# Reordered steps in the four later chunks of an mLSTM cell followed by a GELU MLP

## The chip, the cores and the metric

The kernel runs on one core of one Trainium2 chip. The metric is the device time of one execution in microseconds (us), from the kernel's start on the core to its end. It is written in Bass with the Tile framework, but its order is its own: the tile pools and semaphores are Tile's, while every instruction stands on its engine's queue in the order in which the program issues it (`tc.manual_schedule()`). Five engines have such a queue: PE (TensorE: matrix products and transposes), DVE (VectorE), ACT (ScalarE), POOL (GpSimd) and SP (SyncE, which here only starts DMA transfers). An engine takes its queue strictly in order; a wait for another engine is a semaphore in front of the instruction that waits.

## What is computed

Two blocks, one behind the other. The first is an mLSTM cell on 4 batches, 8 heads, 768 time steps and head size 40:

```python
C, n, m = 0, 0, -1e30
for t in range(768):                      # every batch and head
    m_new  = max(f[t] + m, i[t])
    f_stab = exp(f[t] + m - m_new)
    i_stab = exp(i[t] - m_new)
    C = f_stab * C + i_stab * outer(v[t], k[t])
    n = f_stab * n + i_stab * k[t]
    h = C @ q[t]
    y[t] = sigmoid(o[t]) * h / max(abs(n . q[t]), 1)
    m = m_new
```

Its output, 3072 tokens of 320 numbers (8 heads x 40), goes through an MLP: `h = x @ w_in` (320 to 2048), `g = 0.5 * h * (1 + erf(h / sqrt(2)))`, `out = g @ w_out` (2048 to 320), all in float32.

## The kernel before, in words

*The cell.* The 768 steps are cut into six chunks of 128. Within a chunk the recurrence is written as matrix products: scores of keys with queries, weighed by a matrix W of exponentials (with a mask), times the values; to that comes a product of the queries with the state that the chunk before has left. Of each chunk the four batches (0 to 3) are handled one by one or in pairs (0, 1 and 2, 3).

*The MLP.* A chunk makes 512 tokens (4 batches x 128). They are multiplied by w_in in four groups of four tiles of 128 hidden features (16 tiles); each tile goes through the GELU, and then the 16 tiles are multiplied by w_out and summed in four PSUM accumulators, one per batch. To keep the precision of float32, operands are split: `x_hi`, `x_rest`, `x_low` for the input (six products for the up projection), a whole and two parts for g (three products for the down projection).

*The interleaving.* Chunk 0's MLP has a form of its own. For chunks c = 1 to 5 the MLP of chunk c is mixed with the cell of chunk c + 1, so that TensorE has matrix products of the MLP to do while the other engines work on the cell. The order is written out by hand, in strings of words; `play()` (L1019) runs through the string from left to right and issues each word's instructions, on whichever engines it uses. A word is a letter and a number: the batch, or the tile or group of the MLP. A batch number of 4 or more belongs to the cell one chunk further on (M4 is the mask of batch 0 of cell c + 2). SECOND is played for chunk 1, LATER for chunks 2, 3 and 4, and LAST for chunk 5, which has no cell beside it. Because each engine's queue is in program order, a word's place in the string is its place on every engine that it uses, and two words which share no engine don't order one another.

The words that matter here, with their engine, their lines and what they write:

| word | what it does | engine, line |
|---|---|---|
| U, u | up projection of a group, first part and rest | PE L966, L977, into `pu` |
| g | GELU of one tile: `g_whole`, a part, difference, cast | ACT L984, L985; DVE L986, L987 |
| d | down projection of one tile, 12 matmuls, all four batches | PE L991, into `po` |
| E | output of the chunk before: copy out of `po`, send | ACT L1015 to `o_sb`; SP |
| K, Q | transposes of keys, queries | DVE L512 |
| M, W | mask; exponentials | POOL L474; ACT L500 |
| G | output gate, tanh | ACT L506 |
| D | values times their weights | POOL L539 |
| C0, h0 / C2, h2 | read the state for a pair; update the state for the pair | PE L621 (64 matmuls); PE L632 (32), DVE L639 and L647, POOL L643 |
| S0, S2 | scores of a pair, 64 matmuls; weighing by W | PE L568; DVE L574 |
| V0 to V3 | values of one batch, 64 matmuls, and the sum with the state's part | PE L674 into `ph`; DVE L678 |
| Y | the division and the gate | DVE L685 to L690 |
| t | copy of the last 64 columns of y, twice | ACT L699 |
| X | transpose of y for the MLP ("turn") and its first part | PE L708 (3 transposes) into `px`; ACT L718 to `x_hi` |
| R | `x_rest` and `x_low` from `px` and `x_hi` | DVE L727, L728 |
| L, B, J, O, j, o | loads of blocks of keys and queries, of W's exponents, and of keys, values, gates | SP |
| + | next of the copies of keys and queries to a DRAM scratch `kq_d` | SP |
| Z, a, b | pieces of the splitting of w_in and w_out | ACT, DVE |

*What sets the order around the change.* Dependences that an order must keep: C2 needs the transposed queries (Q2, Q3) and the state; h2 needs the weighed values (D2, D3) and stands behind C2, whose banks `pf` it shares; V2 and V3 need the scores' products (S2) and write into the banks that S0's scores used, and their sum on DVE needs h2's `far`; Y needs V; t and X need Y; X2 and X3 write `px` into the banks of C2 and h2; R needs X. The next chunk's U0 reads `x_hi`, `x_rest` and `x_low` of all four batches. The banks that S2 and C2 write are ones that the up projection's groups use too, so that they must wait until the last GELU of a group (g11, g15) has read its bank. The buffers of g's parts are reused after some tiles, so a g waits for an earlier d.

In code the two steps that the change moves furthest on TensorE, `later_values` (V) and `update_two` (h), are:

```python
for hip in range(2):
    for p in range(NP):
        for r in quarters:
            nc.tensor.matmul(ph[hip][r, p, :], Pm[:, 2 * p + hip, r], vb[turn_of(n)][:, 2 * p + hip, :], ...)
```

```python
nc.tensor.matmul(banks[i][used[hip], H + p, :], k_later[turn_of(c * B + b)][:, 2 * p + hip, :], vw[:, 2 * p + hip, :], ...)
```

The functions that play the strings, with their lines:

## Time and profile before

| what | value |
|---|---|
| time, median of 3 runs | 438.67 us (437.14 to 439.19) |
| the profiled execution: its time, its span | 438.46 us, 436.7 us |
| PE matmuls, busy | 427.3 us, 98% of the span, 5472 instructions |
| PE weight loads, busy | 374.6 us, 86% |
| DVE busy | 296.0 us, 68% |
| ACT busy | 277.3 us, 63% |
| POOL busy | 48.8 us, 11% |
| granted TensorE clock | 1.00, the whole span |

How to read the profile. One execution was recorded. The *span* is from the first to the last recorded instruction; the time of the execution is longer by what lies around it, 438.46 - 436.7 = 1.8 us here. *Busy* time is the time in which an engine has an instruction at work; PEld is the loading of weights into TensorE's array, which overlaps the matmuls (PE). A row of the *groups* gives a line of the kernel, engine, operation, output <- inputs with their sizes, how many, and the mean time. The *chain of waits* goes back from the last instruction, at each step to what released it, and so shows what carries the end; shown in order of time, a row is start, length, engine, tile, line and count, in us. A row "issue" is time in which an engine waited for nothing that the profile shows. The *timeline* lists single instructions, or runs of equal ones, in a stretch of time: start, duration, engine, line, operation; in square brackets stands the idle time before it and what ended it. The *table by stretches* has one row for a stretch from A to B: its length, then the busy time and, in brackets, the number of instructions of PE, PEld, DVE, ACT and POOL, then the granted clock, the busy share of the DMA engines and GB/s. PEldq is the queue of TensorE's instructions, as its sequencer works it off.

### The profile page before, as it was taken

To read this page: it belongs to the slowest core of one execution; us is meant where nothing else is said; L and a number is where in the kernel's file an instruction comes from. 1 tells how busy PE (TensorE), PEld (TensorE's weight loads), DVE (VectorE), ACT (ScalarE), POOL (GpSimd) and SP (SyncE) were. 2 spreads that over 40 slices of the span, in tenths; PEclk is the share of its full clock that TensorE was granted. 3 is DMA by queue.
4 is the path that set the end of the run, shared out by engine and by line. 5 is a ranking of instruction groups with operands and counts; after the bars stand their busy time and mean duration, and the time that the engine had idled before them with its cause. 6 is when DMAs were issued, how large, how long until landed. Compare 5 with 4: busy or idle time off the path is not lost.

```text
span 436.7 us, 13291 instructions
## 1 busy us (share of the span) xinstructions
PE 427.3 (98%) x5472; PEld 374.6 (86%) x5472; DVE 296.0 (68%) x680; ACT 277.3 (63%) x595; POOL 48.8 (11%) x77
## 2 busy tenths in 40 slices
PE   8989999999999999999999999999999999999996
PEld 7777888877988899988899988899988889979986
DVE  8797687797888697747597747597746586533330
ACT  4989999856889985228785229785247715243441
POOL 3001030000430041030041030040010000000000
PEclk9999999999999999999999999999999999999999
DMA  7999994577791592662492653571561400010001
GB/s 151 220 214 243 233 256 87 138 211 179 229 154 56 106 176 60 115 179 50 84 187 42 123 158 60 117 134 32 110 156 17 62 2 2 22 42 2 1 2 60
DMA packets 162268, 48.83 MB, mean 112 GB/s; under 512 B 147776, under 2 KB 155232, under 8 KB 162208
## 3 DMA queue, kind: packets, MB, share of 16 engines
q1 hardware_dynamic: 161888, 47.65, 50.1%
q8 instruction: 43, 0.70, 0.6%
q10 hardware_dynamic: 320, 0.33, 0.2%
q14 instruction: 17, 0.14, 0.1%
HBM read 43.84 MB, written 9.37 MB: 122 GB/s over the span
## 4 chain that ended last, share of the span: by engine, by line
PE 73%; DVE 2%; ACT 2%; DMA 1%; issue 1%; ACTq 0%
PE po L991 31%; PE pu L966 24%; PE pu L977 7%; PE ps L568 3%; PE pf L621 2%; PE ph L674 1%; PE po L888 1%; PE po L674 1%; PE px L708 1%; DMA bits<-in_moe_w_out_dram 1%; PE pf L632 1%; DVE pow L416 1%; DVE w_out L419 0%; ACT w_out_part L935 0%; ACT g_part L873 0%
## 5 line engine op out<-in xcount | busy, mean ns | idle before, releaser
L991 PE MATMUL po<-w_out_part,g_parts 128*128 128x320 f32 x960 | 140.7, 303 | 0.0
L991 PEld LDWEIGHTS po<-w_out_part,g_parts 128*128 128x128 f32 x960 | 131.6, 189 | 5.9 <-issue 4.6
L986 DVE TENSOR_TENSOR g_parts<-g_whole,g_parts 128x512 fp32r<-128x512 f32 x80 | 57.0, 713 | 58.1 <-ACT g_parts L985 56.0
L984 ACT ACTIVATE g_whole<-pu 128x512 f32<-128x512 f32 x80 | 47.1, 589 | 74.2 <-PE pu L977 63.7
L985 ACT ACTIVATE g_parts<-g_whole 128x512 fp32r<-128x512 f32 x80 | 50.5, 631 | 8.3 <-PE po L991 5.1
L474 POOL TENSOR_SCALAR_AFFINE_SELECT W<-W 128x1024 f32<-128x1024 f32 (+2 forms) x20 | 21.7, 1088 | 189.2 <-DMA W<-M_d 154.4
L500 ACT ACTIVATE W<-W,aT 128x128 f32<-128x128 f32 x128 | 38.8, 389 | 0.3
L987 DVE CAST g_parts<-g_whole 128x512 fp32r<-128x512 f32 x80 | 36.2, 453 | 0.0
L699 ACT COPY far<-ob 128x128 f32<-128x128 f32 x16 | 4.6, 290 | 32.9 <-DVE ob L690 32.9
L966 PE MATMUL pu<-x_hi,w_in_hi 128*128 128x512 f32 x80 | 24.2, 384 | 0.0
L966 PE MATMUL pu<-x_hi,hi_first 128*128 128x512 f32 x80 | 24.0, 381 | 0.1
L966 PE MATMUL pu<-x_rest,hi_first 128*128 128x512 f32 x80 | 23.8, 379 | 0.0
L966 PE MATMUL pu<-x_rest,w_in_hi 128*128 128x512 f32 x80 | 23.8, 379 | 0.0
L966 PE MATMUL pu<-x_low,w_in_lo 128*128 128x512 f32 x80 | 23.8, 379 | 0.0
L966 PE MATMUL pu<-x_low,w_in 128*128 128x512 f32 x80 | 23.8, 379 | 0.0
L888 PE MATMUL po<-w_out,g 128*128 128x320 f32 x80 | 22.0, 432 | 0.0
L404 ACT ACTIVATE sig<-bits 128x320 f32<-128x320 f32 (+1 forms) x26 | 15.2, 586 | 10.4 <-issue 6.1
L574 DVE TENSOR_TENSOR W<-ps,W 128x256 f32<-128x256 f32 (+1 forms) x48 | 17.7, 414 | 4.2 <-PE ps L568 3.2
L888 PEld LDWEIGHTS po<-w_out,g 128*128 128x128 f32 x80 | 15.0, 190 | 5.9
L639 DVE TENSOR_TENSOR far<-pf,gT 128x164 f32<-128x164 f32 x32 | 8.4, 319 | 16.1 <-PE pf L632 11.7
L416 DVE SCALAR_TENSOR_TENSOR pow<-sig,pow 128x320 uint32<-128x320 uint32 (+1 forms) x26 | 15.4, 592 | 4.3 <-ACT pow L405 4.3
L1015 ACT ACTIVATE o_sb<-po 128x320 f32<-128x320 f32 x20 | 7.5, 443 | 16.7 <-PE po L991 16.7
(196 smaller groups left out, 778.9 us busy)
## 6 DMA issues: line engine op xcount, KB each, us to landing
W<-M_d SPq DMA_DIRECT2D x16, 512.0 KB, 6.5
bits<-in_moe_w_in_dram SPq DMA_DIRECT2D x20, 256.0 KB, 4.2
bits<-in_moe_w_out_dram SPq DMA_DIRECT2D x16, 320.0 KB, 4.6
blocks<-kq_d SPq DMA_DIRECT2D x32, 128.0 KB, 3.5
ob<-in_o_gate_dram SPq DMA_DIRECT2D x24, 160.0 KB, 4.1
out_dram<-o_sb SPq DMA_DIRECT2D x36, 80.0 KB, 2.0
wide<-M_d SPq DMA_DIRECT2D x4, 512.0 KB, 4.8
kq_d<-in_k_dram SPq DMA_DIRECT2D x6, 320.0 KB, 4.6
```

Source lines behind the costliest of these rows:

```text
L416: nc.vector.scalar_tensor_tensor(out=p, in0=s, scalar=3, in1=p, op0=OP.logical_shift_left, op1=OP.bitwise_or)
L474: nc.gpsimd.affine_select(out=x, in_=x, compare_op=OP.is_ge, fill=1.0e30, base=base, pattern=[[0, H], [1, x.shape[2]]], channel_multiplier=-1)
L500: nc.scalar.activation(out=W[n][:, h, :], in_=src, func=AF.Exp, scale=-1.0, bias=aT[:, self.c, r:r + 1])
L574: nc.vector.tensor_tensor(out=w[r, :, t], in0=ps[i][hip][r, :, t], in1=w[r, :, t], op=OP.mult)
L888: nc.tensor.matmul(to, xs[k][:, b * L:(b + 1) * L], w, start=(n == 0 and k == 0), stop=(n == NF - 1 and k + 1 == len(xs)), skip_group_chec ...
L966: nc.tensor.matmul(in_pairs(pus[i][e]), w3(at[k])[n][:, e, i * P:(i + 1) * P], in_turns(x3[n][:, k, :]), start=(n == 0 and k == 0), stop=F ...
L977: nc.tensor.matmul(in_pairs(pus[i][e]), w3(r)[n][h, p % 2, i * P:(i + 1) * P], in_turns(x3[n][h, NX, :]), start=False, stop=(n == 2), skip ...
L984: nc.scalar.activation(out=whole, in_=self.pus[n // 4][n % 4 // 2][n % 2], func=AF.Gelu)
L985: nc.scalar.activation(out=hi, in_=whole, func=AF.Copy, scale=PART)
L986: nc.vector.tensor_tensor(out=rest, in0=whole, in1=hi, op=OP.subtract)
L987: nc.vector.tensor_copy(out=low, in_=whole)
L991: nc.tensor.matmul(in_pairs(self.po[t]), x[:, t * L:(t + 1) * L], in_turns(w), start=(n == 0 and k == 0), stop=(n == NF - 1 and k == 2), s ...
```

## The change

Only the strings LATER and SECOND change; no instruction is added or removed on any engine apart from waits. As to the words:

- TensorE: V3 and V2 (in this order, where it was V2, V3) stand right behind C2 and h2, and d11 behind them; before, d11 stood between h2 and V2. X3 stands behind d14; before, X2 and X3 stood together ahead of d14.
- DVE: Q3 and K3 ahead of g9's operations (K3 itself behind d4 in the string); g7's operations behind S0's; Y1 before Y0; R1, C2 and h2's operations ahead of g15's; R2 and R3 both behind X3.
- ACT: the output gates in the order G3, G1, G2, G0 and ahead of W3, W2 (in LATER); t1 before t0.
- POOL: D1, M2, D0, M3 ahead of h0's operations (in LATER); before, D0, D1, h0's, M2, M3.
- The outputs E0 to E3 of the chunk before are mixed with K1 and Q1 ahead of u0 (in LATER); before they stood behind u0.
- "+" (the copies to `kq_d`) stands one or more words earlier in some places.

```diff
--- before.py
+++ after.py
@@ -36,16 +36,15 @@
 for at, first, key in ((HI_AT, 10, "h0"), (LO_AT, 10, "h1"), (HI_AT, 13, "b0"), (LO_AT, 13, "b1"), (HI_AT, 0, "b2"), (LO_AT, 0, "b3")):
     at.update((first + i, (key, i)) for i in range(3))
 LATER = """
- U0 u0 E0 E1 E2 E3 K1 Q1 L2 D0 D1 C0 h0 M2 M3 g0 g1 g2 g3 +
- U1 u1 g4 d0 g5 d1 g6 d2 g7 S0 d3 K2 Q2 L3 W2 W3 G0 G1 G2 G3 +
- U2 V0 V1 u2 g8 d4 g9 K3 Q3 B4 B5 J0 J1 d5 g10 d6 g11 S2 L4 d7
- U3 u3 + M4 M5 Y0 Y1 D2 D3 K4 W4 W5 g12 t0 d8 g13 t1 d9 g14 X0 X1 R0 d10 g15 R1 C2 h2 O0 O1 d11 V2 V3 Y2 t2 B6 J2 d12 Y3 t3 Q4 L5 B7 d13 X2 X3 R2 d14 R3 d15 + O2 O3"""
+ U0 E0 K1 E1 E2 Q1 E3 u0 L2 D1 M2 D0 C0 M3 h0 g0 g1 g2 g3 + U1 u1 g4 d0 g5 d1 g6 d2 S0 g7 K2 d3 Q2 L3 G3 G1 G2 G0 W3 W2
+ + U2 V0 V1 u2 g8 Q3 d4 K3 g9 B4 d5 B5 J0 J1 d6 g10 g11 S2 L4 d7 U3 + u3 M4 M5 D2 Y1 D3 Y0 K4 W4 W5 d8 g12 t1 g13 t0 d9 g14
+ X0 X1 R0 d10 R1 C2 h2 O0 g15 O1 V3 V2 Y2 d11 t2 B6 J2 d12 Y3 Q4 t3 L5 B7 d13 X2 d14 X3 R2 R3 + O2 O3 d15"""
 
 SECOND = """
- U0 u0 j2 o0 o1 K1 Q1 L2 M0 M1 D0 D1 W0 W1 a0,3 b0,3 a3 b3 a4,2 b4,2 a6,2 b6,2 C0 h0 M2 M3 g0 g1 g2 g3 o2 o3 + +
- U1 u1 Z Z Z g4 d0 g5 d1 g6 d2 g7 S0 d3 K2 Q2 L3 W2 W3 G0 G1 G2 G3 Z Z +
- U2 V0 V1 u2 + g8 d4 g9 K3 Q3 B4 B5 J0 J1 d5 g10 d6 g11 S2 L4 d7
- U3 u3 + M4 M5 Y0 Y1 D2 D3 K4 W4 W5 g12 t0 d8 g13 t1 d9 g14 X0 X1 R0 d10 g15 R1 C2 h2 O0 O1 d11 V2 V3 Y2 t2 B6 J2 d12 Y3 t3 Q4 L5 B7 d13 X2 X3 R2 d14 R3 d15 + O2 O3"""
+ U0 u0 j2 o0 o1 K1 Q1 L2 M0 M1 D0 D1 W0 W1 a0,3 b0,3 a3 b3 a4,2 b4,2 a6,2 b6,2 C0 h0 M2 M3 g0 g1 g2 g3 o2 o3 + + U1 u1 Z Z Z g4
+ d0 g5 d1 g6 d2 g7 S0 d3 K2 Q2 L3 W2 W3 G0 G1 G2 G3 Z Z + U2 V0 V1 u2 + g8 Q3 d4 K3 g9 B4 d5 B5 J0 J1 d6 g10 g11 S2 L4
+ d7 U3 + u3 M4 M5 D2 Y1 D3 Y0 K4 W4 W5 d8 g12 t1 g13 t0 d9 g14 X0 X1 R0 d10 R1 C2 h2 O0 g15 O1 V3 V2 Y2 d11 t2 B6 J2 d12 Y3 Q4
+ t3 L5 B7 d13 X2 d14 X3 R2 R3 + O2 O3 d15"""
 
 LAST = """
  U0 u0 E0 E1 E2 E3 g0 g1 g2 g3 U1 u1 g4 d0 g5 d1 g6 d2 g7 d3 
```

## The prediction

> **What bounds the kernel now.** I read the page first, then the chain of waits in order of time, then single stretches. From the page:

> ```profile
> span 436.7 us, 13291 instructions
> PE 427.3 (98%) x5472; PEld 374.6 (86%) x5472; DVE 296.0 (68%) x680; ACT 277.3 (63%) x595; POOL 48.8 (11%) x77
> q8 instruction: 43, 0.70, 0.6%
> ```

> TensorE is busy for 98% of the span. The last line matters later: one queue brings nothing but instructions, 43 packets and 0.70 MB. TensorE's 5,472 matmuls and 5,472 weight loads, divided by 43, give 254 a packet, so I read it as TensorE's program arriving in blocks of 256 instructions. The chain of waits in order of time (start, length, work) at the place that the change reorders, in chunks 1 to 4:

> ```profile
> 171.57 1.07 PE pf L621 x64
> 172.65 0.74 PE pf L632 x32
> 173.39 1.83 PE po L991 x12
> 175.22 1.48 PE ph L674 x120
> 176.69 0.35 issue
> 177.04 0.27 PE ph L674 x3
> 177.31 3.46 PE po L991 x24
> 180.76 0.69 PE px L708 x6
> 181.46 3.26 PE po L991 x24
> ...
> 237.38 1.07 PE pf L621 x64
> 238.45 0.74 PE pf L632 x32
> 239.19 1.83 PE po L991 x12
> 241.02 1.51 PE ph L674 x117
> ...
> 304.77 1.83 PE po L991 x12
> 306.59 1.50 PE ph L674 x114
> ```

> From here to the end nothing but TensorE carries the time, so a change that adds no matmul gains or loses by TensorE's gaps alone. There is one large gap: 0.35 us inside the values (L674) of chunk 1, put down to "issue", that is, to no wait the profile knows. The timeline shows where it falls:

> ```profile
> 175.90 0.79 PE L674 MATMUL ph<-vb,wide 128*32 128x41 f32 x61
> 177.04 0.14 PEld L674 LDWEIGHTS ph<-vb,wide 128*32 128x32 f32 x3 [0.47 <-issue]
> ```

> 61 of 64 matmuls of one batch have gone, all with the same operands; the last three come 0.47 us late. No operand can be missing there. I take it that TensorE ran out of fetched program. The table by stretches, cut at every 256th instruction counted on from that gap:

> ```profile
> 174.65:177.04 2.39, 2.04 (x130) 1.71 (x129) 1.96 (x7) 0.00 (x0) 0.00 (x0) 1.00 0.04 9
> 177.04:238.39 61.35, 61.35 (x757) 54.95 (x757) 40.93 (x95) 38.96 (x84) 9.07 (x12) 1.00 0.56 116
> 238.39:241.90 3.51, 3.51 (x130) 3.24 (x129) 3.47 (x11) 0.00 (x0) 1.46 (x3) 1.00 0.04 9
> 303.22:306.92 3.70, 3.70 (x141) 3.43 (x136) 3.67 (x11) 0.00 (x0) 1.06 (x2) 1.00 0.19 36
> 367.57:371.10 3.53, 3.50 (x140) 3.16 (x132) 2.89 (x8) 0.00 (x0) 0.00 (x0) 1.00 0.02 5
> ```

> In each row the counts after the second and third number are matmuls and loads. The block that ended in a gap was used up in 2.39 us, gap included; the three like blocks of chunks 2 to 4 lasted 3.5 to 3.7 us and show no gap. (The second row is the six blocks between: 1,514 and some twenty waits of the sequencer's own.) The sequencer reads ahead of the array:

> ```profile
> L674 PEldq EVENT_SEMAPHORE  x4: 51/51/51, 173.1 to 175.8; - x4
> L632 PEldq EVENT_SEMAPHORE  x1: 51/51/51, 238.4 to 238.4; - x1
> ```

> In chunk 1 it came to the values at 173.1, where the block that ran dry begins, and the next block was there at 177.04: 3.9 us after it entered the block before.

> **The change part by part.** Instruction counts are the same on every engine; SP's order is unchanged row for row, so "+" a step sooner and the copies of the output (E) before u0 move nothing: 0.

> *Values before d11 (chunks 1 to 4).* TensorE ran C2 (64), h2 (32), d11, values (128), d12, d13; now values follow h2 and d11 joins d12 and d13. In instructions C2, h2 and values are 128 + 64 + 256 = 448 without the 24 slow ones of d11 between, which took 1.83 us. Where a block now begins in C2 or h2 it ends in the values 1.83 us sooner, less about 25 value instructions (25/256 of 1.50 = 0.15): in 3.51 - 1.7 = 1.8 us in chunk 2, 3.70 - 1.7 = 2.0 in chunk 3 and, in chunk 4 (no h2), 3.53 - 1.7 = 1.8. Every such block is shorter than the one that ran dry. The wait: at least up to 2.39 us, so 0.6, 0.4 and 0.6; at most up to where the block is known to have been there, 3.51, 3.70 and 3.53, so 1.7 each. I take values towards the upper end, 1.4, 1.2 and 1.2: in chunk 2 the sequencer was at h2 only at 238.4, and 3.9 us from there is past 241.9; in chunks 3 and 4 the block starts inside C2, behind the slow d10, and the sequencer was there somewhat before the array. In chunk 1 the block begins with the values: they would now run from 173.4 to 174.9, and the block ends 19 instructions into d11, at 0.2 + 9.5 x 0.136 = 1.5 us (3.26/24 = 0.136 each), 176.3. The wait for 177.04 is 0.7; the gap it replaces cost 2.09 - 1.50 = 0.6 (175.22 to 177.31 against chunk 3's values). Net +0.1, at worst +0.8, at best -0.6. Sum: 0.1 + 1.4 + 1.2 + 1.2 = +3.9; ends 1.0 and 5.9.

> [...]

> *X2 d14 X3 d15 in place of X2 X3 d14 d15.* A pair of turns takes 0.69 to 0.71 in chunks 1 to 4, some 0.05 of it X3's wait for its copy t3, which now has d14 (1.63) to cover it. Two borders between wide and small matmuls are added, and one goes where d11 joins d12. By the rows a stretch of d costs 0.2 beyond its matmuls (1.83 against 3.26/2 = 1.63), so a border costs 0 to 0.2. Per chunk: -0.05 - 0.2 for the lost one, +0 to 0.4. I take -0.1, four times: -0.4; ends -1.0 and +0.6. X3's parts (x_hi, R3) are now due at the next U0:

> ```profile
> 311.57 0.30 ACT L699 COPY far<-ob 128x128 f32<-128x128 f32 x1 [1.15 <-DVE ob L690]
> 311.91 0.87 ACT L718 ACTIVATE x_hi<-px 128x384 fp32r<-128x384 f32 x2
> 313.84 0.55 DVE L728 CAST x_low<-px 128x384 fp32r<-128x384 f32 x1
> 315.36 0.59 PE L966 MATMUL pu<-x_hi,w_in_hi 128*128 128x512 f32 x2
> ```

> X3 comes one d (1.63) later, so its x_low ends near 314.39 + 0.9 = 315.3, and U0 reads it only as its third operand, 0.87 after its start at 315.4: hidden, by about 1 us. If that cover is gone, 0.5 a chunk.

> *Vector order.* R1 and h2's work now go ahead of g15's two operations, which only d15 needs; Q3 and K3 go ahead of g9's. The second delays g11's GELU, since its buffer is g9's, and the scores S2 need the bank that this GELU reads. Chunk 4:

> ```profile
> 349.60 0.58 ACT L984 ACTIVATE g_whole<-pu 128x512 f32<-128x512 f32 x1
> 350.59 0.65 DVE L986 TENSOR_TENSOR g_parts<-g_whole,g_parts 128x512 fp32r<-128x512 f32 x1
> 351.62 1.57 PE L568 MATMUL ps<-qT,kT 64*64 64x128 f32 x64
> 286.34 1.31 DVE L987 CAST g_parts<-g_whole 128x512 fp32r<-128x512 f32 x1
> ```

> g9's cast now ends where g10's first operation began, 350.6; GELU 0.6 after it, 351.2; S2 at 351.62: 0.4 to spare. A cast beside POOL took 1.31 instead of 0.42, as in the last row; if it hit g9's cast, 0.9 - 0.4 = 0.5 in each of chunks 2 and 3. I take 0. g7 behind S0 puts K2, Q2 and the loads that they release 1.1 later (0.69 + 0.42); their data are used more than 3 us after.

> *ScalarE and POOL.* The gates before W3, W2: same work, same two table loads, with ACT idle behind them. Masks M2, M3 before h0's decay on POOL:

> ```profile
> 248.99 0.83 SPq L210 DMA_DIRECT2D wide<-M_d  x1
> 257.35 0.93 POOL L643 TENSOR_TENSOR state<-state,dec 128x164 f32<-128x164 f32 x2 [8.62 <-PE pf L621]
> ```

> The mask's load takes about 4.8 us from 248.99 and M3 1.8: 255.6, before 257.35. 0; up to 1 us if it lands late.

> **Sum.** 3.9 - 0.4 = +3.5 on the profiled execution's 438.46 (0.2 under the median 438.67 of the runs shown): 441.9.

> **The rivals.** (1) *The fetch never binds*, and the gap of chunk 1 was something else, which stays: 438.46 - 0.4 = 438.1. For it: three like blocks of chunks 2 to 4 show no gap. Against it: those were all 1.1 us longer than the one that shows it. It decides if a block arrives within 1.8 us of the one before. [...] (2) *Full price*: each wait reaches its upper end, 1.7 x 3 + 0.1 - 0.4: 443.3. (3) *The fetch is quick, but S2 waits* behind a slowed cast in chunks 2 and 3: 438.46 - 0.4 + 1.0 = 439.1. (4) *Low price*: 0.6 + 0.4 + 0.6 + 0.1 - 0.4: 439.8. (5) *Faster*: chunk 1's gap goes as well and borders cost nothing: 438.46 - 0.6 - 1.0 = 436.9; more is not there, as TensorE has no other idle time.

> **How the numbers follow.** Fetch waits of 1.2 to 1.4, or the full price: 0.62. Low price 0.13; (1) 0.15, as the fetch is read from a single gap; (3) 0.05; (5) 0.05. 0.5% is 2.2 us, about what a measurement of this kernel can tell from no change: slower means above 440.9. From the cases: slower 0.65, the 0.62 and the upper part of the low price; the rest of it, (1), (3) and some of (5) are the same, 0.32; faster 0.03. The likeliest case alone is 440.7 to 443.5. With (1) left out the range would miss more than 2 in 10, so it starts at 437.9, just below (1), and ends at 443.8, above the full price.

> **What would show it.** Right: in the chain after, gaps put down to "issue" of about 1 us in the values of chunks 2 to 4, in the middle of one batch's 64 matmuls, and one in chunk 1 just inside d11; PE's busy time as before, its share of the span lower. Wrong: values of 1.5 us with no gap. Gaps before S2 (L568) released by ACT would speak for (3); gaps at U0 released by DVE L728, for the turns.

## The result, and the profile after

The changed kernel takes 440.86 us in the median of 8 runs (439.82 to 441.65), the kernel before 438.58 us in 8 runs (436.9 to 439.24). The ratio is 1.0055, with a 95% interval of 1.0039 to 1.0071: slower by 2.3 us. The profiled execution took 441.31 us, 2.85 us more than that of before. Line numbers of the changed kernel are one lower than before (L673 for L674).

The head of the page after; the columns are as in the table of before:

```profile
span 439.5 us, 13266 instructions
PE 426.1 (97%) x5472; PEld 374.1 (85%) x5472; DVE 294.9 (67%) x680; ACT 278.0 (63%) x595; POOL 48.9 (11%) x77
```

TensorE does the same 5,472 matmuls in the same busy time (1.2 us less), in a span that is 2.8 us longer. The time went into gaps. The chain of waits of the kernel after, in order of time (start, length, work), at the values of chunks 1 to 4:

```profile
174.82 1.42 PE po L990 x9
176.35 3.83 PE po L990 x27
...
238.57 1.08 PE ph L673 x92
239.66 1.44 issue
241.10 0.50 PE ph L673 x23
241.60 5.09 PE po L990 x36
...
305.99 0.67 PE ph L673 x56
306.66 0.89 issue
307.56 0.94 PE ph L673 x58
...
370.49 0.93 PE ph L673 x73
371.41 1.13 issue
372.54 0.67 PE ph L673 x49
```

Three gaps put down to "issue", of 1.44, 0.89 and 1.13 us, stand in the values of chunks 2, 3 and 4. In chunk 1 the gap has become 0.1 us (174.82 + 1.42 = 176.24, and the next piece starts at 176.35) and has moved into d11, behind 9 of its 12 matmuls. The single instructions around the gap of chunk 2, from the timeline:

```profile
239.15 0.51 PE L673 MATMUL ph<-vb,W 128*32 128x41 f32 x32
241.10 0.39 PE L673 MATMUL ph<-vb,W 128*32 128x41 f32 x21 [1.44 <-issue]
```

On both sides it is the same batch's products with the same operands (the window cuts the second run, of 32, after 21), and all 64 of a batch write one bank, so no operand, bank or engine can have been late.

I numbered TensorE's instructions in the program in order (two for each matmul with its weights, one for each wait of its own) and set them against the 5,472 matmuls of the trace. The first late matmul is number 4,799 in chunk 1, 6,591 in chunk 2, 8,384 in chunk 3 and 10,176 in chunk 4. Divided by 256 these leave 191 or 192 each, as does the 4,800 of the one gap before. The gaps stand on the grid of the blocks in which TensorE's program arrives. In the table by stretches of the kernel after, cut at these borders (length, then PE, PEld, DVE, ACT and POOL busy and count, clock, DMA share, GB/s):

```profile
173.38:176.35 2.97, 2.86 (x137) 2.66 (x136) 2.92 (x10) 0.00 (x0) 0.00 (x0) 1.00 0.13 37
237.82:241.10 3.28, 1.84 (x131) 1.66 (x129) 2.73 (x9) 0.00 (x0) 0.58 (x2) 1.00 0.02 5
304.49:307.56 3.07, 2.18 (x142) 1.96 (x133) 2.11 (x8) 0.00 (x0) 0.93 (x2) 1.00 0.19 36
369.60:372.54 2.94, 1.81 (x142) 1.64 (x133) 2.44 (x8) 0.00 (x0) 0.00 (x0) 1.00 0.03 6
```

In chunks 2 to 4 TensorE has work for 1.8 to 2.2 us in the block, and the next block is there 2.9 to 3.3 us after the array has entered this one. (The 2.39 us of chunk 1 before don't speak against that: there the sequencer had gone through d11 ahead of the array and entered the block at 173.1.)

The trace has the packets of the queue q8 too. From 238.8 to 239.9 us, ahead of the gap of chunk 2, its DMA view has one (packets, MB, share of 16 engines):

```profile
q8 instruction: 1, 0.02, 5.4%
```

This packet runs from 238.86 to 239.81, and the late products begin 1.28 us after its end. The packets ahead of the gaps of chunks 1, 3 and 4 end at 175.16, 306.08 and 371.20, 1.2 to 1.5 us before the first late instruction. Over all ten profiles of this study there are 21 gaps of 0.1 us or more on the grid from chunk 1 on, and each ends 1.2 to 1.6 us after its packet has. At the borders without a gap the packet had ended at least 1.6 us before its block was needed, with one exception, in the second experiment. Before the change it was 1.41 us at the gap of chunk 1, and 1.8 to 1.9 us at the three like borders of chunks 2 to 4, which have no gap of 0.1 us. So the gaps are waits for these packets. In the kernel after, the packets started 0.4 to 1.0 us after the array had entered the block before; why this varies is not known, and it sets much of a gap's size.

There is one more loss, in chunk 3, ahead of its last up projection (U3). The timeline of DVE, PE and POOL:

```profile
286.51 1.58 DVE L985 TENSOR_TENSOR g_parts<-g_whole,g_parts 128x512 fp32r<-128x512 f32 x1
288.35 1.57 DVE L985 TENSOR_TENSOR g_parts<-g_whole,g_parts 128x512 fp32r<-128x512 f32 x1
289.85 0.88 DVE L986 CAST g_parts<-g_whole 128x512 fp32r<-128x512 f32 x1
291.52 0.67 PE L965 MATMUL pu<-x_hi,hi_first 128*128 128x512 f32 x2 [0.68 <-DVE W L573]
286.26 1.29 POOL L473 TENSOR_SCALAR_AFFINE_SELECT W<-W 128x1024 f32<-128x1024 f32 x1 [27.31 <-DVE g_parts L985]
288.06 2.38 POOL L473 TENSOR_SCALAR_AFFINE_SELECT W<-W 64x1024 f32<-64x1024 f32 x2 [0.51 <-DMA W<-M_d]
```

DVE's work for g10 and g11 ran beside POOL's masks: the subtraction took 1.58 us twice (0.69 when alone, from 283.11), the cast 0.88 (0.42). The weighing of the scores S2 stands behind it on DVE, and U3 waits 0.68 us for the bank that this weighing reads. Before, the same place lost 0.08 us.

The ledger by chunks, from the first product of a chunk's up projection to that of the next (before, from the chain: 118.85, 184.72, 249.96, 315.52, 379.39):

| | chunk 1 | chunk 2 | chunk 3 | chunk 4 | sum |
|---|---|---|---|---|---|
| before | 65.87 | 65.24 | 65.56 | 63.87 | 260.54 |
| after | 65.36 | 66.51 | 66.89 | 64.71 | 263.47 |
| difference | -0.51 | +1.27 | +1.33 | +0.84 | +2.93 |

The work ahead of chunk 1 (118.74 us against 118.85) and chunk 5 are almost unchanged.

### The profile page after: what moved, and what is told of

Read it like the earlier page. It is cut to its first block, busy times and chain, and to the rows that moved or that the text cites. A ratio compares the mean times of both kernels' runs of the same rounds, so it can differ in the third digit from the quotient of the medians.

```text
span 439.5 us, 13266 instructions
## 1 busy us (share of the span) xinstructions
PE 426.1 (97%) x5472; PEld 374.1 (85%) x5472; DVE 294.9 (67%) x680; ACT 278.0 (63%) x595; POOL 48.9 (11%) x77
## 4 chain that ended last, share of the span: by engine, by line
PE 84%; DVE 5%; ACT 4%; issue 2%; SPq 2%; DMA 1%; DVEq 0%; ACTq 0%
PE po L990 30%; PE pu L965 24%; PE pu L976 7%; PE po L887 5%; PE pu L786 2%; PE ps L567 2%; PE pf L620 2%; PE px L707 2%; PE pu L817 2%; DMA ob<-in_o_gate_dram 1%; PE ph L673 1%; PE po L673 1%; SPq L174 1%; PE pf L631 1%; ACT W L499 1%
## 5 line engine op out<-in xcount | busy, mean ns | idle before, releaser
L984 ACT ACTIVATE g_parts<-g_whole 128x512 fp32r<-128x512 f32 x80 | 50.5, 631 | 6.7 <-PE po L990 3.5
L986 DVE CAST g_parts<-g_whole 128x512 fp32r<-128x512 f32 x80 | 35.9, 448 | 0.0
L404 ACT ACTIVATE pow<-bits,low_bits 128x320 uint32<-128x320 uint32 (+1 forms) x26 | 17.4, 669 | 0.0
```

The costliest lines, as they stand in the source:

```text
L404: nc.scalar.activation(out=p, in_=lo, func=AF.Relu, scale=0.9 * 2.0 ** -29, bias=low_bits)
L984: nc.scalar.activation(out=hi, in_=whole, func=AF.Copy, scale=PART)
L986: nc.vector.tensor_copy(out=low, in_=whole)
```

## The experiments

The theory (F): TensorE's program comes in blocks of 256 instructions, the next one is there about 3 us after a block is entered, and the change makes blocks that are used up sooner. Its rivals: the other moves of the change made the loss (O), or the dense run C2, h2, V stalls for a reason of its own, wherever it stands in the program (D).

### The values moved, and nothing else

```diff
- ... C2 h2 O0 O1 d11 V2 V3 Y2 t2 ...
+ ... C2 h2 O0 O1 V2 V3 Y2 d11 t2 ...
```

(the kernel before, in both strings)

> The kernel before, with V2 and V3 (both in their old order) put ahead of d11 in the two strings, and nothing else. If the program's arrival carries the loss (theory F), the gaps of the changed kernel come with this move alone: gaps put down to issue in the values of chunks 2, 3 and 4 of about 1.4, 0.9 and 1.1 us, against the one of 0.35 us in chunk 1 before, less 0.2 us a chunk because d11 joins d12: about 441.1 us. If the loss came from the other moves (vector order, turns, gates; theory O), this is the time of before, 438.6, or 437.8 with d11 joined.

Measured: 441.3 us against 438.42, ratio 1.0066 (1.004 to 1.0093). From its chain of waits, the gaps of chunks 2, 3 and 4:

```profile
239.78 0.80 issue
...
305.62 1.25 issue
...
371.02 0.20 issue
371.22 0.34 PE ph L674 x9
371.56 0.65 issue
```

This one move has the whole loss: O falls. The gaps on the grid are of 0.80, 1.25 and 0.65 us where 1.4, 0.9 and 1.1 had been expected; in chunk 2 the packet started 0.6 us after the array had entered the block before, against 1.0 in the kernel after. In chunk 4 there are two gaps, and only the second is on the grid (number 10,175). The first is a wait for the bank: the timeline puts it down to R1's cast on DVE (L728), which ends at 371.02 there, since in this kernel g15's operations still stand ahead of it. The change had moved R1 ahead of g15, and its own profile has no such wait.

### d11 put back

```diff
- ... C2 h2 O0 g15 O1 V3 V2 Y2 d11 t2 ...
+ ... C2 h2 O0 g15 O1 d11 V3 V2 Y2 t2 ...
```

(the kernel after, in both strings)

> The changed kernel with d11 put back ahead of V3 and V2, all its other moves kept. F: the gaps of chunks 2 to 4 are gone and the small one of chunk 1 is back; what is left of the loss is the wait of U3 in chunk 3 (0.6 us), less 0.05 us a chunk for the turns apart: 438.6 to 439.2 us. O: still about 440.9.

Measured: 438.17 us against 438.42, ratio 0.9989 (0.997 to 1.0008). No gap on the grid in any of chunks 1 to 4; they take 65.34, 65.11, 65.09 and 63.57 us. From its chain:

```profile
240.97 1.43 PE ph L673 x116
242.40 3.46 PE po L990 x24
245.86 0.33 PE px L707 x3
246.19 1.63 PE po L990 x12
247.82 0.33 PE px L707 x3
248.15 1.63 PE po L990 x12
```

The values take 1.43 us without a break. F had expected the small gap of chunk 1 back, and U3's wait with it, hence 438.6 to 439.2; this profile has neither. The array used up the block of chunk 1 in about 1.9 us without a gap. The sequencer had again run ahead through d11 (it came to the values at 173.6, the array at 175.7), and the packet ended at 175.70, 1.33 us before its block was needed: just in time. Before the change, TensorE had stood idle for the last 0.35 of the 1.41 us. So the time that the array spends in a block is only part of the account; what lies just ahead of the block, and when the packet starts, count too.

The other moves cost nothing that can be told here, and gain a little: X2 d14 X3 d15 takes 0.33 + 1.63 + 0.33 + 1.63 = 3.92 us, against 0.71 + 3.26 = 3.97 before.

### The same order, the borders elsewhere

```diff
-    fill(76)
+    fill(94)     # first run: 72 instructions more
+    fill(124)    # second run: 192 instructions more
```

(the kernel after; `fill` makes small products at the very start, which nobody reads)

> The changed kernel with 18 more of the small products at the very start, which nobody reads: 72 more TensorE instructions ahead of everything, no order changed, so every border of 256 instructions falls 72 instructions earlier in the work. F: in chunks 3 and 4 a border now falls near the middle of C2, h2 and the values, and the blocks on both sides take over 3.2 us: no gap there. In chunks 1 and 2 a block still lies almost whole in them: gaps of about 1.3 us each, after about 102 of the 128 matmuls of the values in chunk 1 and 61 of 128 in chunk 2. Sum of the gaps 2.7 against 4.3 us: about 439.3 us. Rival D, by which the dense run itself stalls (its operands, banks or the array, 1 to 1.6 us behind h2): the gaps stay at their places and sizes, 440.9.

> The same with 48 more small products, 192 more instructions. F: the borders fall badly: a gap of 1.1 us after 43 of 128 matmuls of the values in chunk 1, 1.7 at the end of the values of chunk 2, 1.3 after 88 of 128 in chunk 3, 1.7 after 111 of 128 in chunk 4, and up to 1 us at the end of the values V0, V1 of chunks 3 and 4, which have none now: 6.3 to 7.6 us in all against 4.3: 443 to 444 us. D: gaps as now, 440.9.

Measured: 441.68 us (ratio 1.0065, 1.0042 to 1.0087) with 72 more, and 445.96 us (1.0186, 1.0148 to 1.0223) with 192 more. The times are not the 439.3 and the 443 to 444 that F had given, but the gaps are at its places; by the time alone, 72 more would speak for D's 440.9. With 72 more instructions, the chain in chunks 1 and 2:

```profile
174.52 1.25 PE ph L673 x92
175.77 1.80 issue
177.57 0.49 PE ph L673 x27
...
242.57 0.72 PE ph L673 x61
243.29 1.21 issue
244.49 0.93 PE ph L673 x56
```

By their numbers (4,799 and 6,592) the gaps came after 102 and 61 matmuls of the values, as expected, but that of chunk 1 is 1.80 us long and not 1.3 (its packet started 1.1 us after the array had entered the block before). Chunks 3 and 4 have none and take 64.86 and 63.49 us, 2.0 and 1.2 us less than in the changed kernel, where chunk 3 has the wait of U3 too. With 192 more, four gaps:

```profile
177.62 0.81 issue
...
244.43 1.71 issue
...
310.58 1.25 issue
...
375.64 1.51 issue
```

They stand at numbers 4,799, 6,847, 8,639 and 10,432, all on the grid, within two or three tenths of the expected sizes; the two further ones at the end of V0, V1 did not come. D, by which the gaps would have stayed where they were in the work, falls.

Two things made the times longer than expected. With 192 more, the start itself runs dry: the timeline there has

```profile
2.77 2.24 PE L255 MATMUL cold<-w_out 128*32 128x41 f32 x123
6.57 0.43 PE L255 MATMUL cold<-w_out 128*32 128x41 f32 x25 [1.55 <-issue]
```

The small products are dense too (123 in 2.24 us, against 128 of the values in 1.5), and in the midst of them the next block is 1.55 us late (number 447, on the grid too; its packet ended 1.5 us before). By the start of its first product, chunk 1 begins at 122.43 us, against 118.58 in the kernel after: 3.85 of the 4.3 us between the two profiles are lost there, so the time of this run says little of the gaps in the values. With 72 more it begins at 119.78 us, and U3 of chunk 2 waits 0.81 us for DVE, in the way of chunk 3 above. With the 0.5 us of the longer gap that makes 2.5, by which its profiled execution (441.84 us) lies above 439.3; three of its twelve runs took under 439.5.

### d11 between the two batches

```diff
- ... O1 V3 V2 Y2 d11 t2 ...
+ ... O1 V3 d11 V2 Y2 t2 ...
```

(the kernel after)

> The changed kernel with d11 between V3 and V2 instead of behind both. F: what counts is what a block of 256 instructions holds between two borders. In chunk 1 the block has 107 instructions of V3, d11 and 125 of V2 (0.6 + 1.8 + 0.7 = 3.2 us), in chunk 2 3.5 and in chunk 4 3.4 us, each with d11 inside: no gap, or 0.2 in chunk 1. In chunk 3 it has 77 of C2, 65 of h2 and 114 of V3, 2.0 us: one gap of about 1.1 us there, at the end of V3. About 439.3 us. D: behind every h2 the values follow as closely as in the changed kernel, so each chunk keeps a wait in V3, half of the present ones or more: 440 to 441.

Measured: 439.58 us, ratio 1.0027 (1.0014 to 1.0039). From the chain, chunk 3:

```profile
306.26 0.67 PE ph L673 x56
306.93 1.17 issue
308.10 0.28 PE ph L673 x8
```

One gap of 1.17 us in chunk 3, behind 56 of V3's 64 matmuls, 0.10 us in chunk 1 and none in chunks 2 and 4: what F had given, from nothing but a count of instructions. In this profile, that of the slowest of the twelve runs (441.06 us), U3 of chunk 3 also waits for DVE, 1.3 us.

### Q3 and K3 behind g9

```diff
- ... g8 Q3 d4 K3 g9 B4 ...
+ ... g8 d4 g9 Q3 K3 B4 ...
```

(the kernel after)

> The changed kernel with Q3 and K3 behind g9, as before the change (in the order Q3, K3). If the wait of U3 in chunk 3 (0.67 us before the first matmul, ended by the weighing of the scores on DVE) came from these two standing ahead of g9, it goes in every chunk, and the gaps of the values stay as they are (about 0.1, 1.4, 0.9, 1.1): 440.3 us. If it is only POOL's mask that happens to run beside DVE then, it can still come: 440.9.

Measured: 441.02 us, ratio 1.0053 (1.0036 to 1.0069): no difference to the kernel after that can be told. In its profile U3 of chunk 3 loses about 0.1 us, as it did before the change, and the gaps of the values are 1.10, 1.17 and 0.96 us. Over all ten profiles: with Q3 and K3 behind g9 (four profiles) the longest wait of U3 is 0.1 us. With them ahead of g9 (six) there are three longer ones, 0.7 (after, chunk 3), 0.8 (72 more, chunk 2) and 1.3 us (the one just above, chunk 3), and none in the other chunks. In these three POOL's first mask begins 5.2 to 5.9 us ahead of U3, and three or four of DVE's operations are slowed; in the others it begins at most 4.6 us ahead, and at most two are. The wait itself is part of that lead, though: without it the lead is 4.4 to 4.6 us. The four profiles with Q3 and K3 behind g9 have a lead of 4.3 to 4.6 us in chunk 3 too, and lose at most 0.1. With the two ahead of g9, the wait came in the three chunks with a lead over 4.4 us and in none of the others, with 4.3 or less. So an early mask alone is not enough, and the counts fit that it takes this order on DVE as well. But the medians don't show it (441.02 against 440.86 us), and no run moves the masks alone: this stays open.

### No block used up early

```diff
-    fill(76)
+    fill(26)
```

(once in the kernel after with d11 put back, once in the kernel before)

> d11 ahead of the values as in the second experiment, and 50 of the 76 small products at the start left out, 200 TensorE instructions fewer, so that by theory F no block of 256 is used up in under 3.2 us in any of the four chunks: no gap at all from chunk 1 to the end, also not by chance. Chunks 1 to 4 at 65.3, 65.1, 65.1 and 63.6 us (against 65.9, 65.2, 65.6 and 63.9 before); the start may gain or lose some tenths by the shorter warming of TensorE: 437.2 to 438.2 us.

> The kernel before with the same 50 small products left out. F: its one gap, 0.35 us in the values of chunk 1, goes, since the border there falls 200 instructions later in the work; chunk 1 takes 65.4 us instead of 65.9, the others stay at 65.2, 65.6 and 63.9: about 438.1 us if the start is unchanged. D: the gap stays, 438.4.

Measured: 437.71 us with d11 put back, ratio 0.9983 (0.9966 to 0.9999), and 438.51 us for the kernel before, 1.0001 (0.9988 to 1.0015). Neither has a gap on the grid from chunk 1 on. The values of chunk 1 in the kernel before, with the small products left out:

```profile
176.66 1.49 PE ph L674 x113
178.16 3.46 PE po L991 x24
```

Its chunk 1 takes 65.29 us instead of 65.87, as F had given, and the others 65.22, 65.28 and 63.84. The time itself lies nearer to D's 438.4; the gap that went speaks for F. In this profile the start gave the gain back: chunk 1 began at 120.14 us, 1.45 later than before. Over the profiles with an unchanged start it began between 118.52 and 119.46, so part of that is the spread of the start, and what fewer small products do to it can't be read from one profile; that they warm TensorE, as the expectation has it, was an estimate, and no run shows it. The first version, with chunks of 65.27, 65.15, 65.05 and 63.57 us, is the fastest of this study: 0.2% under the kernel before, with an interval that ends just short of no change.

## Why the prediction was right, and where it was off

It forecast 441.9 us (437.9 to 443.8) and slower with a chance of 0.65. The measured 440.86 us lie at the lower end of the likeliest case (440.7 to 443.5), on the border of 440.9 that the prediction set for slower; the interval of the ratio (1.0039 to 1.0071) leaves out no change. The mechanism is shown; that the total came out so near is partly luck, as the terms show.

- *The bound.* Right: from chunk 1 on, only TensorE's gaps and what it waits for made a difference.
- *Values before d11.* The mechanism was right in sign, place and cause: blocks of 256 instructions run dry. The first, second and fourth experiments and the two shifted runs show it from five sides. The terms were 0.1, 1.4, 1.2 and 1.2 us for chunks 1 to 4. Counted in the same way, as what the stretch takes beyond 1.50 us of values (in chunk 1 beyond the 5.09 of d11 to d13), the profile has 0.27 in place of 0.59 in chunk 1, so -0.3, then 1.53, 1.01 and, in chunk 4, 1.22 in place of 0.13, so 1.1. The sum is +3.3 where the prediction had +3.9. The step that was mis-sized most is chunk 1: it set the arrival of the block at the same instant as before, 177.04, but it came at 176.35. The array had entered the block before it at 173.38, not 174.65, and the packet started 0.47 us sooner. The place was right almost to the instruction: 19 instructions, 9.5 matmuls, into d11 were expected, 9 matmuls were seen. The ends held: the 2.9 to 3.3 us after which the next block was there lie between the 2.39 that had run dry and the 3.5 to 3.7 that had not.
- *The turns apart, d11 joined to d12.* The step said -0.1 a chunk, because it left 0 to 0.4 for two new borders between wide and small products. They cost nothing (0.33 a turn), and the lost border gave its whole 0.2 (d11 to d13 take 5.09 us against 1.83 + 3.46). So -0.25 a chunk, -1.0 in all where the sum had -0.4: the lower end of its range.
- *Vector order.* The step put 0 on it, on the ground that g11's GELU had 0.4 us to spare for S2. S2 indeed did not wait (its products ran from 287.45 to 289.02, right behind d6). The wait came one step further on, at U3, which needs S2's weighing done on DVE: +0.6 in the profiled execution. The prediction followed the delay to S2 and not on to the next writer of that bank. The profiled execution (441.31 us) is the second slowest of the eight; how often the others have this wait is not known.
- *ScalarE, POOL, outputs and "+"*: 0, and nothing in the profile speaks against that.
- *The sum.* +3.3 - 1.0 + 0.6 = +2.9, as in the ledger (2.93; the spans differ by 2.8, the medians by 2.3), against +3.5 predicted. All three terms were off by 0.6 us, two of them downwards and one upwards.
- *The rivals.* That the fetch never binds (438.1) is refuted here for dense runs of small matmuls: 0.65 to 1.8 us at a border. The three like blocks of chunks 2 to 4 before, which lasted 3.5 to 3.7 us, show no gap of 0.1 us or more at their border, and neither do the other borders from chunk 1 on. The third rival, DVE slowed beside POOL, came true in part, at another place and in addition to the main case.

## What to carry to other kernels

## What had not been expected of the hardware

- In each of the 21 gaps from chunk 1 on, TensorE did not go on when the packet of the next block had ended, but 1.2 to 1.6 us later.
- The small products at the start, which nobody reads, can run dry like the values: with 192 more of their instructions there is a gap of 1.55 us among them, on the grid too, and chunk 1 began 3.85 us later.
- DVE's subtraction on 128x512 takes 0.69 us alone and up to 1.6 us beside POOL's masks, the cast 0.42 and up to 1.3 us. Which of DVE's operations meet them differs from chunk to chunk and from profile to profile.
